# Windowed attention and a squared-ReLU MoE on one core: the first six P V products turned, the last first-product by Strassen, finer token units, another plan

## The chip, the cores and the metric

The kernel runs on one core of a Trainium2 chip. The metric is the device time in microseconds of one execution. Five engines take part: TensorE (PE, matrix products), VectorE (DVE), ScalarE (ACT), GpSimd (POOL, here it only issues loads that convert float32 to bf16) and SyncE (SP, here it only issues DMA transposes). Each engine works through its own list of instructions in order, and engines wait for one another by semaphores.

## What is computed

Two stages in a row: attention in a sliding window of 32 positions to either side, over 8 batches, 8 heads, 576 positions and 64 dimensions; then, on the 4608 tokens of 512 features that come out, two products with a squared ReLU between them.

```python
scores = scale * np.matmul(q, k.transpose(0, 1, 3, 2))
mask = np.abs(pos[:, None] - pos[None, :]) <= window
scores = np.where(mask, scores, -1000000000.0)
attn = np.exp(scores - np.max(scores, axis=-1, keepdims=True))
attn = attn / (np.sum(attn, axis=-1, keepdims=True) + 1e-09)
x = np.matmul(attn, v)             # -> [4608, 512]
h = x @ w_in                       # [512, 2048]
r = np.maximum(h, 0.0)
out = (r * r) @ w_out              # [2048, 512]
```

## The kernel before

**Attention** goes in 24 steps `G` of 192 queries (three to a batch). Keys and queries of a step are loaded by POOL (`load_qk`, L357), turned so that the head dimension lies on the partitions (`turn_pe` on the PE for the first two batches, `turn_dma` by DMA transposes on SP for the others), and multiplied in two windows of 128 keys, `w` = 0 and 1 (`scores`, L465). ScalarE takes the exponential. For steps 0 to 2 the mask is added in the PE as a bias; for the others DVE multiplies by it (L515). The probabilities lie in `pt`, keys on partitions, queries in columns, eight heads beside each other.

`pv` (L519) multiplies with `pt` as the weights and the values as the moving side, 65 columns a head: 64 of values and one of ones, which gives the sum of the row. So queries come out on partitions, and one reciprocal of 8 sums (L550) with a multiplication of 512 columns (L553) a window normalises them into `xa` and `xb`. The MoE needs them the other way, features on partitions, in the ring `xt` of 1536 tokens. `xturn` (L558) does that: for steps 0 to 5 by eight PE transposes (L570, L575) and one eviction by ScalarE (L580), for the others by two DMA transposes on SP (L584, L587).

**The MoE's first product** (`mm1`, L592) fills one PSUM bank of 512 columns at a time (`ht`, two of them): a unit is 192 tokens by 2 feature blocks up to token 768, 256 by 2 up to 1024, and 512 by 1 after that. ScalarE takes the ReLU into `rt` (four of them), DVE squares it into the ring `gt` of 1024 tokens (L614). **The second product** is plain for the first 512 tokens (`mm2`, L618, matmuls at L625). From there each 512 tokens are a 2 x 2 block product by Strassen's scheme with seven products (`strassen`, L694; matmuls at L687). DVE makes its sums of weights once (`sums_w2`, L648) and its sums of `gt` for every tile (`sums_g`, L663).

**The order of the work** is written out by a planner at build time. Every operation is recorded with an engine, what it reads and writes, an assumed duration and a key; `schedule` (L92) plays it through and gives each engine a fixed list. Keys of the attention steps are `3 * G + OG[G] - LEAD`, of their loads `3 * G + OL[G] - LEAD - AHEAD`, of the Strassen tiles `8 * g + LS + OS[g]`; the first product's key is its first token over 64. `move=(rounds, ns)` is a DMA's assumed length. Loads from the third batch on may also not be issued before the PE operation that had last been recorded (`after=self.moe`). In the gaps that the plan shows for the PE before 40 us it inserts matmuls on zeros (L294).

The constants that the change touches:

```python
NSPLIT = 6     # steps whose two windows are scored one after the other
NXT = 6        # steps whose result is turned on the PE
LEAD = 10.0
def dve(n, fast=True):
    return 153 + (0.52 if fast else 1.04) * n
```

Of the kernel before, what the change touches and what calls it, by code (L numbers as in the profile page):

```python
# [5 lines left out]
ALU = mybir.AluOpType  # L6
# [12 lines left out]
RING = 1536  # L19
GRING = 1024  # L20
NSTD = 4
BIAS = 74.0
LS = 10.75
OG = [-0.75, -0.25, -2.0, -2.75, -0.25, 2.25, 4.0, 1.25, 2.0, 1.75, 3.0, 0.75, 0.25, -0.25, -0.5, 0.25, -0.5, -2.0, -2.25, -3.0, 2.75, 1.25, -4.25, 3.0]
OL = [3.0, 1.0, 4.5, 5.5, 2.5, -0.5, -2.0, -3.5, -3.5, -0.5, 0.0, -0.5, -1.0, -3.5, -1.5, 1.5, -0.5, -3.5, -3.5, -1.0, 2.0, 1.0, -3.0, -6.5]
OS = [-4.0, 4.5, -2.0, 2.0, 1.75, 3.25, 4.5, 5.25, 4.5]
NV, NRAW = 6, 6
NTURN = 2
NXT = 6
LEAD = 10.0  # L30
# [19 lines left out]
class Prog:  # L50
# [11 lines left out]
    def rec(self, eng, fn, reads=(), writes=(), dma=None, dur=100, key=0.0, move=0, name="", after=None, slack=0):  # L62
        op = Op()
        op.eng, op.fn, op.dma, op.dur, op.key, op.move, op.name = eng, fn, dma, dur, key, move, name
        op.deps, op.order = set(), set()
        op.inc, op.val, op.sem = False, None, None
        op.slack = slack
        op.lat = self.LAT[eng]
        for r in reads:
            w = self.writer.get(r)  # L70
            if w is not None:
                (op.order if w.eng == eng == "PE" else op.deps).add(w)
        for t in writes:
            w = self.writer.get(t)
            if w is not None:
                (op.order if w.eng == eng and w.dma is None and dma is None else op.deps).add(w)
# [12 lines left out]
        self.ops.append(op)  # L89
        return op  # L90

    def schedule(self):  # L92
# [37 lines left out]
        def serve(until):  # L130
            nonlocal now, spent
            while now < until:
# [117 lines left out]
class Gen:  # L250
# [5 lines left out]
    def alloc(self):  # L256
# [11 lines left out]
        self.MASK = [sb(f"mask{i}", [128, 128], BF16) for i in range(4)]  # L268
        self.BIAS = [sb(f"bias{i}", [128, 128], BF16) for i in range(4)]
        self.ID = sb("ident", [128, 128], BF16)  # L270
        self.E = [sb(f"e{i}", [128, 1024], BF16) for i in range(2)]
        self.PT = [sb(f"pt{i}", [128, 8, 128], BF16) for i in range(3)]
        self.RS = [sb(f"rs{i}", [128, 8], F32) for i in range(4)]
        self.XA = [sb(f"xa{i}", [128, 512], BF16) for i in range(3)]
# [7 lines left out]
        self.UE = [sb(f"ue{i}", [128, 512], F32) for i in range(2)]  # L282
        self.RT = [sb(f"rt{i}", [128, 512], BF16) for i in range(4)]
# [29 lines left out]
    def setup_mask(self, i, key):  # L313
# [19 lines left out]
        else:  # L333
            p.writer[hi[0]] = last
            p.readers[hi[0]] = []

# [110 lines left out]
    def turn_dma(self, t, b, g, key):  # L447
# [14 lines left out]
    def mask_of(self, g, w):  # L462
        return w if not (g == 0 and w == 0 or g == 2 and w == 1) else w + 2

    def scores(self, G, ws):  # L465
# [8 lines left out]
        def f(e):  # L474
            for w in ws:
                k0 = a + 128 * w
                mi = self.mask_of(g, w)
# [5 lines left out]
                for j in range(4):  # L483
                    for par in range(2):
                        r = 64 * par
                        q = qt[r:r + 64, j, a + 64:a + 192]
                        if w == 0:
# [10 lines left out]
        rd += ["id"] + [("bias", self.mask_of(g, w)) for w in ws] if pm else []  # L498
# [3 lines left out]
        for w in ws:  # L502
            n = 2 * G + w
            sc = self.AT[:, 1024 * reg[w]:1024 * reg[w] + 1024]
            e_, pt = self.E[n % 2], self.PT[n % 3]
            if pm:
                self.p.rec("ACT", lambda e, pt=pt, sc=sc: e.activation(pt[:].rearrange("p h q -> p (h q)"), sc, ACTF.Exp, scale=0.125),
                           reads=tags[w], writes=[("pt", n % 3)], key=key, dur=act(1024), name=f"X{G}{'AB'[w]}")
# [3 lines left out]
            mi = self.mask_of(g, w)  # L512
# [3 lines left out]
                       reads=[("e", n % 2), ("mask", mi)], writes=[("pt", n % 3)], key=key, dur=dve(1024),  # L516
                       name=f"M{G}{'AB'[w]}")

    def pv(self, G, w):  # L519
# [3 lines left out]
        reg = 1 if G < NSPLIT else 0  # L523
        c0 = 1024 * reg
        vt, pt, avp = self.V[G % NV], self.PT[n % 3], self.AT
# [13 lines left out]
        rd = [("v", G % NV, w), ("vset", G % NV), ("pt", n % 3), "zz"]  # L539
# [17 lines left out]

    def xturn(self, G):  # L558
# [3 lines left out]
        wr = [("xt", (3 * G + c) % (RING // 64)) for c in range(3)]  # L562
        if G < NXT:
            ps, bank = self.AT[:, 1024:1536].bitcast(BF16), self.half(2)
            if G < 3:
                ps, bank = self.OUTP[0][:].bitcast(BF16), ["outp0"]

            def f0(e):
                for j in range(4):
                    mm = e.transpose(ps[:, 192 * j:192 * j + 64], xa[64:128, 128 * j:128 * j + 128], self.ID[64:128, 64:128])  # L570
                return mm

            def f1(e):
                for j in range(4):
                    mm = e.transpose(ps[:, 192 * j + 64:192 * j + 192], xb[:, 128 * j:128 * j + 128], self.ID[:])  # L575
                return mm

            self.p.rec("PE", f0, reads=[("xa", G % 3), "id"], writes=bank, key=key, dur=150, name=f"T{G}a")
            self.p.rec("PE", f1, reads=[("xb", G % 3), "id"] + bank, writes=bank, key=key, dur=230, name=f"T{G}b")
            self.p.rec("ACT", lambda e: e.activation(self.XT[:, :, r:r + 192],  # L580
                                                     ps[:, 0:768].rearrange("p (j q) -> p j q", j=4), ACTF.Copy),
                       reads=bank, writes=wr, key=key, dur=act(768), name=f"XT{G}")
            return
        self.p.rec("SP", lambda e: e.dma_start(self.XT[:, :, r:r + 64], xa[64:128, :], transpose=True),  # L584
                   reads=[("xa", G % 3)], writes=wr[:1], dma=(f"xa{G % 3}", G), key=key - 0.3, dur=TISS, move=(16, 20), name=f"T{G}a",
                   slack=TSLACK)
        self.p.rec("SP", lambda e: e.dma_start(self.XT[:, :, r + 64:r + 192], xb[:], transpose=True),  # L587
                   reads=[("xb", G % 3)], writes=wr[1:], dma=(f"xb{G % 3}", G), key=key, dur=TISS, move=(32, 20), name=f"T{G}b", slack=TSLACK)
# [3 lines left out]
    def mm1(self, t0, n, ds, key):  # L592
# [16 lines left out]
        self.moe = self.p.rec("PE", f, reads=[("xt", s) for s in steps] + [("w1", d0 // 4)], writes=[f"ht{k % 2}"], key=key,  # L609
# [8 lines left out]
    def mm2(self, u, seg, key):  # L618
# [14 lines left out]
        if seg == 3:  # L633
# [4 lines left out]
                       reads=[("oe", u % 4)], writes=[("out", u)], dma=(f"o{u % 4}", u), key=key, dur=600, move=(8, 80), name=f"st{u}")  # L638

    def sums_w2(self, key):  # L640
        w, t, p = self.W2, self.TS, self.p
        for c in range(2):
            k, k8 = slice(4 * c, 4 * c + 4), slice(8 + 4 * c, 12 + 4 * c)
            b11, b12, b21, b22 = w[:, k, 0:256], w[:, k, 256:512], w[:, k8, 0:256], w[:, k8, 256:512]
            for i, a, b, rd in ((0, b12, b11, [("w2", c)]), (2, b22, b12, [("w2", c), ("w2", 2 + c)]),
# [3 lines left out]
                      writes=[("t", i, c)], key=key, dur=dve(1024), name=f"w{i}{c}")  # L649

# [43 lines left out]
    def strassen(self, g, key):  # L694
# [5 lines left out]
        def out(i, j, rd, fn, eng, k, name):  # L700
# [7 lines left out]
                  writes=[("out", u)], dma=(f"o{u % 4}", u), key=k, dur=600, move=(16, 45), name=f"st{u}")  # L708
# [18 lines left out]
    def build(self):  # L727
        p = self.p
        self.k1 = 0
# [6 lines left out]
        self.setup_mask(2, K + 1)  # L736
# [5 lines left out]
        self.setup_mask(0, K + 4)  # L742
        self.setup_mask(3, K + 5)
        for n, i in enumerate((2, 1, 0, 3)):
# [22 lines left out]
        for G in range(NG):  # L767
# [12 lines left out]
            for w in range(2):  # L780
                at(base + 0.3 * w + 0.1, self.pv, G, w)
            at(base + 0.5, self.xturn, G)
        t0 = 0
        while t0 < NTOK:
            n = 192 if t0 < 768 else 256 if t0 < 1024 else 512
            m = 512 // n
            for x, d in enumerate(range(0, 16, m)):
# [54 lines left out]
```

## Time and profile before

| what | us |
|---|---|
| median of three runs | 316.83 |
| the three runs | 310.51, 316.90, 316.83 |
| the profiled execution | 312.76 |
| its span, first to last instruction | 310.8 |
| idle matmuls on zeros (L294), 183 of them | 13.7 busy |
| sixth step's eviction to `xt` (L580) ends | 68.81 |
| last matmul of the first product starts | 286.2 |

Durations of operations that the text uses, mean of one: 

| operation | ns |
|---|---|
| reciprocal, 128x8 from PSUM (L550) | 208 |
| normalising multiplication, 128x512 from PSUM (L553) | 689 |
| mask multiplication, 128x1024 bf16 (L515) | 691 |
| square, 128x384 / 128x512 bf16 (L614) | 355 / 422 |
| sums of 128x1024 bf16 (L648, L663) | 679 to 686 |
| key copy from PSUM, 640 / 768 bf16 columns (L444) | 492 / 558 |
| eviction of `xt`, 128x768 (L580) | 808 |
| ScalarE, 128x512 from PSUM (L611, L698) | 599, 602 |

"Busy" of the PE counts each matmul until its result is written, so neighbouring ones overlap; the pace of a chain of matmuls is read from the start of one to the start of the next. The granted clock is that of the PE, as a share of full speed. In the waits "issue" is time for which the profile shows no releaser.

### The profile page before, as it was taken

How to read it: one execution, taken by the hardware profiler on the slowest of the kernel's cores; microseconds unless marked ns; L12 is line 12 of the kernel's file. 1: busy time of each engine (PE TensorE's matmuls, PEld its weight loads, DVE VectorE, ACT ScalarE, POOL GpSimd, SP SyncE). 2: the span in 40 equal slices, each digit the busy share in tenths (PEclk: the TensorE clock that was granted, in tenths of full speed). 3: DMA queues.
4: the chain of work that ended last, by engine and by line, in shares of the span. 5: the costliest groups of instructions: out<-in, count | busy, mean ns of one | idle time of the engine just before them, and what ended most of it. 6: DMA issues, size and time to landing. Idle time of an engine off the chain costs nothing.

```text
span 310.8 us, 7401 instructions
## 1 busy us (share of the span) xinstructions
PE 292.8 (94%) x2993; PEld 205.6 (66%) x3027; DVE 192.6 (62%) x420; ACT 166.7 (54%) x260; POOL 117.6 (38%) x153
## 2 busy tenths in 40 slices
PE   6899999999799999999999499999979999999995
PEld 6788776868685567556667455586548556666874
DVE  7135766645986896598539636695549765743701
ACT  3546657747536765746675156625762575355230
POOL 8999457308355650299114002992000000000000
PEclk9999999999999999999999979999999999999999
DMA  9999999999999999999999922999974311201123
GB/s 150 167 206 197 187 153 155 190 170 135 143 169 199 157 161 163 94 151 146 173 144 145 210 41 60 123 156 193 169 97 62 88 41 24 71 34 36 64 71 103
DMA packets 179553, 40.37 MB, mean 130 GB/s; under 512 B 166720, under 2 KB 179008, under 8 KB 179520
## 3 DMA queue, kind: packets, MB, share of 16 engines
q0 software_dynamic: 121920, 18.98, 92.7%
q1 hardware_dynamic: 46752, 11.09, 28.1%
q10 hardware_dynamic: 10848, 9.83, 11.4%
q8 instruction: 24, 0.39, 0.5%
q14 instruction: 9, 0.07, 0.1%
HBM read 38.80 MB, written 9.44 MB: 155 GB/s over the span
## 4 chain that ended last, share of the span: by engine, by line
PE 68%; issue 10%; DMA 8%; POOL 6%; DVE 4%; ACT 1%; SPq 1%; POOLq 0%; ACTq 0%; DVEq 0%
PE ht L605 30%; PE outp L687 23%; DMA kraw<-in_k_dram 5%; PE outp L625 4%; PE at L535 4%; PE at L489 3%; POOL kraw L365 2%; POOL qraw L365 2%; POOL v L396 2%; DMA v<-in_v_dram 2%; DMA qt<-qraw 2%; PE outp L294 2%; DVE ss L663 1%; DVE gt L614 1%; ACT rt L611 1%
## 5 line engine op out<-in xcount | busy, mean ns | idle before, releaser
L605 PE MATMUL ht<-xt,w 128*128 128x512 bf16 (+2 forms) x741 | 136.8, 326 | 6.1 <-issue 4.6
L611 ACT ACTIVATE rt<-ht 128x512 bf16<-128x512 f32 (+1 forms) x152 | 86.5, 576 | 74.4 <-PE ht L605 65.4
L605 PEld LDWEIGHTS ht<-xt,w 128*128 128x128 bf16 x768 | 68.6, 98 | 48.7 <-issue 5.6
L614 DVE TENSOR_TENSOR gt<-rt 128x512 bf16<-128x512 bf16 (+1 forms) x152 | 61.5, 408 | 59.0 <-ACT rt L611 56.6
L365 POOL DMA_DIRECT2D kraw<-in_k_dram x46 | 36.2, 809 | 92.6 <-issue 47.6
L510 ACT ACTIVATE e<-at 128x1024 bf16<-128x1024 f32 x42 | 41.4, 1021 | 11.0 <-PE at L489 11.0
L396 POOL DMA_DIRECT2D v<-in_v_dram x48 | 41.5, 891 | 0.1
L515 DVE TENSOR_TENSOR pt<-e,mask 128x1024 bf16<-128x1024 bf16 x42 | 29.0, 691 | 18.3 <-ACT e L510 18.2
L365 POOL DMA_DIRECT2D qraw<-in_q_dram x46 | 36.3, 810 | 0.5 <-issue 0.5
L687 PE MATMUL outp<-w,gt 128*128 128x256 bf16 x256 | 32.2, 273 | 0.7 <-ACT outp L698 0.7
L687 PE MATMUL outp<-ts,ss 128*128 128x256 bf16 x256 | 31.7, 273 | 0.3 <-DVE ss L663 0.3
L687 PE MATMUL outp<-ts,gt 128*128 128x256 bf16 x256 | 31.6, 273 | 0.0
L687 PEld LDWEIGHTS outp<-w,gt 128*128 128x128 bf16 x256 | 24.7, 98 | 7.7 <-ACT outp L698 1.1
L687 PEld LDWEIGHTS outp<-ts,ss 128*128 128x128 bf16 x256 | 24.4, 98 | 5.9 <-DVE ss L663 0.4
L687 PEld LDWEIGHTS outp<-ts,gt 128*128 128x128 bf16 x256 | 24.6, 98 | 4.2
L535 PEld LDWEIGHTS at<-v,pt 128*64 128x64 bf16 (+1 forms) x576 | 17.1, 106 | 12.6 <-issue 4.2
L535 PE MATMUL at<-v,pt 128*64 128x65 bf16 (+1 forms) x576 | 20.8, 196 | 2.8 <-DVE xa L553 1.7
L550 DVE RECIPROCAL rs<-at 64x8 f32<-64x8 f32 (+1 forms) x48 | 10.0, 209 | 15.3 <-PE at L535 14.0
L489 PEld LDWEIGHTS at<-qt,kt 64*128 64x128 bf16 x384 | 10.8, 94 | 11.1 <-issue 10.5
L489 PE MATMUL at<-qt,kt 64*128 64x128 bf16 x384 | 15.9, 218 | 1.8 <-DMA qt<-qraw 1.8
L553 DVE TENSOR_TENSOR xa<-at,rs 64x512 bf16<-64x512 f32 x24 | 16.7, 695 | 0.8
L553 DVE TENSOR_TENSOR xb<-at,rs 128x512 bf16<-128x512 f32 x24 | 16.5, 689 | 0.7
(65 smaller groups left out, 218.6 us busy)
## 6 DMA issues: line engine op xcount, KB each, us to landing
out_dram<-oe ACTq DMA_DIRECT2D x36, 256.0 KB, 4.5
qraw<-in_q_dram POOLq DMA_DIRECT2D x46, 96.0 KB, 8.6
v<-in_v_dram POOLq DMA_DIRECT2D x32, 128.0 KB, 10.6
w<-in_moe_w_in_dram POOLq DMA_DIRECT2D x4, 512.0 KB, 9.4
w<-in_moe_w_out_dram POOLq DMA_DIRECT2D x4, 512.0 KB, 16.6
kraw<-in_k_dram POOLq DMA_DIRECT2D x14, 112.0 KB, 12.9
kraw<-in_k_dram POOLq DMA_DIRECT2D x16, 96.0 KB, 6.0
v<-in_v_dram POOLq DMA_DIRECT2D x16, 96.0 KB, 12.0
```

Of the source, the lines that this page charges most:

```text
L365: self.p.rec("POOL", lambda e, j=j: e.dma_start(raw[0:h, j, :].rearrange("p (h d) -> p h d", h=8), s[:, j]), writes=[("raw", t, G % NRAW, ...
L396: self.p.rec("POOL", lambda e, j=j, lo=lo, hi=hi, k0=k0: e.dma_start(vt[lo - k0:hi - k0, j, :, 0:64], self.v[b, :, lo:hi, :].rearrange("h ...
L489: mm = e.matmul(sc[:, 512 * par + 128 * j:512 * par + 128 * j + 128], kt[r:r + 64, j, k0:k0 + 128], q, start=not pm, stop=True, skip_group ...
L510: self.p.rec("ACT", lambda e, e_=e_, sc=sc: e.activation(e_[:], sc, ACTF.Exp, scale=0.125), reads=tags[w], writes=[("e", n % 2)], key=key, ...
L515: self.p.rec("DVE", lambda e, pt=pt, ee=ee, mb=mb: e.tensor_tensor(pt[:], ee, mb, ALU.mult), reads=[("e", n % 2), ("mask", mi)], writes=[( ...
L535: mm = e.matmul(avp[z:z + n, c:c + 65], pt[:, 4 * (h % 2) + h // 2, z:z + n], vt[:, w, h, 0:65], start=((w == 0 or z == 64) and y == 0), s ...
L553: self.p.rec("DVE", lambda e: e.tensor_tensor(x[r0:128, :].rearrange("p (x y c) -> p x y c", x=2, y=4), av[:, :, :, 0:64], rb, ALU.mult), ...
L605: mm = e.matmul(ht[:, n * x:n * x + n], self.W1[:, ft, 128 * d:128 * d + 128], self.XT[:, ft, r:r + n], start=(ft == 0), stop=(ft == 3))
L611: self.p.rec("ACT", lambda e: e.activation(rt[:, 0:c], ht[:, 0:c], ACTF.Relu), reads=[f"ht{k % 2}"], writes=[("rt", k % 4)], key=key, dur= ...
L614: self.p.rec("DVE", lambda e: e.tensor_tensor(gt[:, d0:d0 + len(ds), rg:rg + n], rr, rr, ALU.mult), reads=[("rt", k % 4)], writes=[("gt", ...
L625: mm = e.matmul(op[:], gt[:, d, r:r + 128], self.W2[:, d, :], start=(d == 0), stop=(d == 15))
L687: mm = e.matmul(op[:, 256 * y:256 * y + 256], lhs[:, l0[0] + k, a:a + 128], rhs[:, r0 + k, c0:c0 + 256], start=start and y == 0 and k == 0 ...
```

## The change

Steps 0 to 5 get `pv_turned` in place of `pv` and `xturn`: the values are the weights, the probabilities move, and the result comes out with features on partitions. A second matmul with a block of ones as the weights gives the sums, repeated on all 64 partitions of the head, so the reciprocal is of 128x384 instead of 128x8. The multiplication writes `xt` directly. The two halves `x` (four heads each) use the same two PSUM banks.

```diff
+    def pv_turned(self, G, x):
+        key = 3 * G + OG[G] - LEAD + 0.3 + 0.1 * x
+        vt, pts, at = self.V[G % NV], [self.PT[(2 * G + w) % 4] for w in range(2)], self.AT
+        bank = self.half(2) + self.half(3)
...
+            for w in range(2):
+                for y in range(2):
+                    for par in range(2):
+                        h = 4 * x + 2 * y + par
+                        c = 192 * y + 64 * w
+                        for z, lhs in enumerate((vt[:, w, h, 0:64], self.ONES[:])):
+                            mm = e.matmul(at[64 * par:64 * par + 64, 1024 + 512 * z + c:1024 + 512 * z + c + 128], lhs,
+                                          pts[w][:, 4 * par + 2 * x + y, :], start=(w == 0 and y == 0), stop=True,
+                                          skip_group_check=True)
...
+        rq = self.RQ[x]
+        self.p.rec("DVE", lambda e: e.reciprocal(rq, at[:, 1536:1920]), reads=bank, writes=[("s", 0, x)],
+                   key=key, dur=dve(384, False), name=f"R{G}{'ab'[x]}")
...
+        self.p.rec("DVE", lambda e: e.tensor_tensor(dst, src, rq.rearrange("p (y q) -> p y q", y=2), ALU.mult),
```

For these steps window 0 takes its queries in their natural order, with two plain masks (4 and 5) beside the four old ones, and `pt` has four buffers instead of three.

The last 512 tokens' first product (`MSTART = 8`) becomes four units of Strassen's seven products, each on two PSUM banks of its own turn (`ht`, then two pairs of `at`). Sums of `w_in` are made once, into the buffers of the loaded keys and queries; sums of `xt` once; the two copies of a unit go to the `e` tiles.

```diff
+            if t0 >= 512 * MSTART:
+                if t0 == 512 * MSTART:
+                    at(t0 / 64 - 1, self.sums_w1, t0 / 64 - 1)
+                at(t0 / 64 - 0.5, self.sums_x, t0, t0 / 64 - 0.5)
+                for x in range(4):
+                    at(t0 / 64 + 2 * x, self.mm1_strassen, t0, 2 * x, x % 3, t0 / 64 + 2 * x + OM[x % 3])
...
+        product(1, ks[0])
+        copy(y, x, xtag, ytag, ks[0], f"sd{t0}.{d}")
+        product(2, ks[1])
+        direct(0, 0, x, xtag, ks[1])
+        product(6, ks[2])
+        copy(u2, y, ytag, [("e", 0)], ks[2], f"u{t0}.{d}")
+        product(5, ks[3])
+        copy(p5, x, xtag, [("e", 1)], ks[3], f"p{t0}.{d}")
+        product(7, ks[4])
+        added(1, 1, y, ytag, p5, [("e", 1)], ks[4])
+        product(3, ks[5])
+        added(0, 1, x, xtag, u2, [("e", 0)], ks[5])
+        product(4, ks[6])
+        direct(1, 0, y, ytag, ks[6])
```

`direct` is the ReLU on ScalarE and the square on DVE as before; `added` is an addition from PSUM and a squared ReLU, both on DVE.

Units of 256 tokens reach to token 2048 (`NFINE`) instead of 1024. The plan's constants are other ones, among them the lead and the assumed lengths of DMAs (`move`), and operations on ScalarE and DVE that overwrite what the same engine wrote or read now wait for it by semaphore.

```diff
-LEAD = 10.0
+LEAD = 11.5
-OG = [-0.75, -0.25, -2.0, -2.75, -0.25, 2.25, 4.0, 1.25, ...
+OG = [-3.75, -10.5, -4.75, -0.25, -3.0, -5.5, -7.5, -2.5, ...
-OL = [3.0, 1.0, 4.5, 5.5, 2.5, -0.5, -2.0, -3.5, ...
+OL = [7.5, 2.0, 5.0, -1.5, -1.0, -1.5, -0.5, 2.0, ...
-LS = 10.75
+LS = 8.25
...
-                if spent >= (120 if now < 30000 else 180 if q == "POOL" else 60):
+                if spent >= (400 if q == "POOL" else 200):
...
-                (op.order if r.eng == eng and r.dma is None else op.deps).add(r)
+                (op.order if r.eng == eng and eng not in ("ACT", "DVE") and r.dma is None else op.deps).add(r)
...
-                       dma=(f"t{t}{G % 6}", G), key=key, dur=TISS, move=(h // 4, 20), name=f"td{t}{b}{g}", slack=TSLACK)
+                       dma=(f"t{t}{G % 6}", G), key=key, dur=TISS, move=(h // 4, 22.6), name=f"td{t}{b}{g}", slack=TSLACK)
```

More of the change, by code (lines that the diff above doesn't have):

```diff
@@ L75, in rec @@
             if w is not None:
[L76 removed]
+                (op.order if w.eng == eng and eng not in ("ACT", "DVE") and w.dma is None and dma is None else op.deps).add(w)
             for r in self.readers.get(t, ()):
[L78 removed]
+                (op.order if r.eng == eng and eng not in ("ACT", "DVE") and r.dma is None else op.deps).add(r)
         if after is not None:
@@ L607, in f @@
             return mm
-        self.moe = self.p.rec("PE", f, reads=[("xt", s) for s in steps] + [("w1", d0 // 4)], writes=[f"ht{k % 2}"], key=key,
+        self.moe = self.p.rec("PE", f, reads=[("xt", s, x) for s in steps for x in range(2)] + [("w1", d0 // 4)], writes=[f"ht{k % 2}"], key=key,
                    dur=4 * len(ds) * (n / 2.4 + 2.5), name=f"A{t0}.{d0}")
@@ L735, in build @@
         self.setup_id(K)
-        self.setup_mask(2, K + 1)
+        self.ms("DVE", ["ones"], self.ONES[:], 1.0, K + 2)
+        self.setup_mask_plain(5, K + 1)
         self.setup_mask(1, K + 2)
```

204 lines of the change are left out of this document (154 added, 50 removed).

## The prediction

> **What bounds the kernel now.** I read the page first: engine shares, then the 40 slices.
>
> ```profile
> PE 292.8 (94%) x2993; PEld 205.6 (66%) x3027; DVE 192.6 (62%) x420; ACT 166.7 (54%) x260; POOL 117.6 (38%) x153
> ...
> PE   6899999999799999999999499999979999999995
> ...
> DVE  7135766645986896598539636695549765743701
> ACT  3546657747536765746675156625762575355230
> ```
>
> TensorE (PE) is the bound as a share, but not in every stage. The first four slices hold idle matmuls on `zz`; slices 23 and 29 (about 179-186 and 225-233 us) hold stalls. So I asked three stages separately: the opening, whose six attention steps the change rewrites; the stalls, which a new plan could move; and the last tile. For the opening, the busy time of each engine in stretches, and the timeline of PE around the sixth step:
>
> ```profile
> core 0: us, PE busy (x) PEld busy (x) DVE busy (x) ACT busy (x) POOL busy (x), PEclk, DMA share, GB/s
> 13.50:24.00 10.50, 10.45 (x177) 8.98 (x178) 4.35 (x10) 5.00 (x8) 10.50 (x14) 1.00 1.29 205
> 24.00:45.00 21.00, 20.89 (x274) 17.53 (x277) 14.18 (x33) 12.74 (x24) 13.78 (x18) 1.00 1.83 180
> 45.00:69.00 24.00, 23.41 (x301) 16.25 (x304) 14.31 (x32) 16.61 (x26) 9.46 (x12) 1.00 2.01 165
> ```
>
> ```profile
> 67.56 0.40 PE L575 MATMUL at<-ident,xb 128*128 128x128 bf16 x4
> 67.80 1.89 PE L625 MATMUL outp<-w,gt 128*128 128x512 bf16 x8
> 69.52 1.91 PE L605 MATMUL ht<-xt,w 128*128 128x256 bf16 x16
> ```
>
> From 13.5 to 69 us VectorE (DVE) is busy 4.35+14.18+14.31 = 32.8 of 55.5 us. The sixth step's `xt` is evicted from 68.00 to 68.81, and the first matmuls that read it start at 69.52, directly after the last L625 of the four plain output blocks: the PE has no other MoE work left. What delays the sixth step's `xt` delays the PE.
>
> The stall, from the timeline:
>
> ```profile
> 178.65 1.22 SPq L587 DMA_TRANSPOSE xt<-xb  x1
> ...
> 179.07 3.08 PE L605 MATMUL ht<-xt,w 128*128 128x512 bf16 x7 [4.28 <-issue]
> ```
>
> A tile's matmuls wait 4.28 us. No releaser is named; an `xt` transpose issued by SP at 170.93 is the last transfer that they need, so I read this as that transfer landing late. The seven matmuls then take 427 ns each by their weight loads (180.35 to 180.77), not 216: the granted clock is 0.89 over 176 to 192 us. Loss: 4.28 + 7 x 0.211 = 5.8 us. A second wait, 1.75 us before the scores at 229.38, names the query transpose.
>
> **The change, part by part.** All against the profiled execution: 312.76 us (span 310.8), which is 1.3% under the median of the three runs (316.83) and above their lowest (310.51).
>
> Turned P V, removed. Per step: two reciprocals and two multiplications on DVE (2 x (0.21 + 0.69) = 1.80 us), eight transposes on the PE and one 0.81 us eviction on ScalarE. Six steps: 10.8 us of DVE.
>
> Turned P V, added. Per half step: 16 matmuls of 128 columns, a reciprocal of 128x384 from PSUM, and a multiplication of 128x384. The multiplication: L553's 128x512 takes 690 ns; the key copies of 768 and 640 elements take 558 and 492, which leaves a fixed part of some 160 ns; so 1.035 ns per element, 160 + 384 x 1.035 = 0.56 us. The reciprocal has only this row:
>
> ```profile
> L550 DVE RECIPROCAL rs<-at 128x8 f32<-128x8 f32 x24 | 5.0, 208 | 4.2 <-PE at L535 3.3
> ```
>
> Eight elements should take 160 + 8 = 168 ns at one element a cycle; they take 208 to 211. The 41 to 49 ns above that are either a longer start, then 384 elements take 0.56 to 0.60 us, or a slope: (209 - 160)/8 = 6.1 ns an element, then 160 + 384 x 6.1 = 2.5 us. I take the slope, 2.5 us, because the fixed part of two other PSUM forms agrees and leaves no room for another; both ends stay for the range. The Trainium skill (VectorE: DVE Perf Modes, "First, the fixed hardware budget") says that Reciprocal runs as an iterative divide with a repeat count of 8; read as eight cycles an element it speaks against this change harder than my row does, and is a rival below.
>
> DVE then carries 12 x (2.5 + 0.56) = 36.7 us instead of 10.8: 32.8 + 25.9 = 58.7 us in a stretch of 55.5. DVE becomes the opening's bound. The order on each engine is fixed by a plan that books 0.55 us for this reciprocal, so nothing is rearranged for it.
>
> When is the sixth `xt` ready? Lower bound, DVE never idle: 13.5 + 58.7 = 72.2, 3.4 us late. Upper bound, nothing absorbed: 12 x 2.16 us (3.06 for 0.90) less six times the removed transposes and eviction (some 1.4 us from L575's start to L580's end): 25.9 - 8.4 = 17.5 late. Between: the first step's second exponential ends at 13.75; two halves of 1.0 (16 matmuls at 56 ns and handover) + 2.5 + 0.56 + 0.1, one after the other as both use one PSUM pair, end at 22.2 where the old eviction ended at 17.9. Steps four to six have scores at 45.2, 51.3 and 59.3, 7 us apart, and each asks DVE for 6.1 + 1.4 (two masks) + 0.56 (keys) + 2.84 (eight squares of 0.355) = 10.9 us. Three such from 45.2, behind some 2 us left over, end at 80: 11 us late. I take 11.
>
> What comes back: PE idles 2.0 us from 69 to 94, and runs no L605 from 80.3 to 93.5, because a 512-token unit needs step eight; the 256-token units need only the next step. I give back 3 us. Net of the opening: +8, bounds 0.4 to 17.5. The extra matmul time (32 x 56 ns against some 0.85 us a step, +0.9) lies in PE waits for DVE; without that cover it is 5 us.
>
> Other edits of the opening. The plain masks and `ones` are a few DVE instructions of 0.1 to 0.3 us before 6 us; the first scores wait for the key copy ending at 9.63, so 0. The self-waits on DVE and ScalarE are for operations long done; a dependent DVE pair shows a gap of 0.03 us, and both engines have idle time: 0. If that cover is gone on DVE in the opening, its 75 instructions there make 2.3 us.
>
> The new plan, 256-token units to token 2048. Unit sizes change no PE time: 16 matmuls of 256 take 1.75 us, 8 of 512 take 1.73. LEAD rises by 1.5 steps, and transposes are planned 13% longer, so `xt` and scores' transfers are issued earlier against the PE. That aims at 5.8 + 1.75 = 7.5 us of stalls. I take 60%, -4.5; bounds: all, -7.5, and a new stall of the middle size, +3, as every load and every queue is reordered (POOL's loads, SP's transposes, ScalarE's stores). What is late next are the scores' own transposes, behind each other on SP at 1.2 us each.
>
> Last tile by Strassen. 64 matmuls of 512 at 216 ns (13.8 us) become 112 of 256 at 109 (12.2) and two of 0.22: -1.2 us. DVE gains 8 x 0.69 + 4 x 0.42 for sums, and per unit 2 x 1.38 + 2 x 0.42 instead of 4 x 0.42: +15 us from about 262 to 286, where it was busy under half. The chain of a unit through the two shared `e` tiles is two copies of 0.60, two products of 0.44 with 0.2 handovers and an add of 0.69: some 3.1 us; four fit in the 21 us in which other products fill the PE. I take -1.2; if that filling runs out, +2.
>
> Sum: 312.8 + 8 - 4.5 - 1.2 = 315.1 us. That is 0.7% over the profiled execution and 0.5% under the median.
>
> **The rivals.**
> (a) The reciprocal runs one element a cycle: 0.56 us. DVE gets +2.6 us, the first `xt` comes at 18.3, the opening loses nothing and the finer units give 2: 312.8 - 2 - 4.5 - 1.2 = 305. For it: nothing in the trace measures the slope. Against: the 41 ns. Chance 0.15.
> (b) The PE's fixed order, slower. The second half's matmuls stand in PE order where the plan expects the first half's multiplication; everything behind them waits too. If each reciprocal's lateness blocks the head of PE's queue, the opening loses the full 17.5 and gives back little (2): 312.8 + 17.5 - 2 - 1.2 = 327 with stalls that stay, 323 with half of them gone. It decides once the plan has under 2 us of other PE work between the halves. For: L625 stands directly before L605 with nothing spare. Against: from 45 to 69 us some 8.0 us of L605 and 10.4 us of L625 stood between the steps, and can cover such a wait. Chance 0.24.
> (c) The stalls stay or move: 315.1 + 4.5 = 319.6. Chance 0.15.
> (d) Eight cycles an element: 8 x 1.035 x 384 + 160 = 3.34 us, 0.84 more each, 10 us on a DVE that is full: 325. Against: eight elements would then take 226 ns and take 209. Chance 0.06. [...]
> My forecast holds 0.40; its own range is 308 to 322.
>
> **How the numbers follow.** Two per cent (6.3 us) is about what a measurement of this kernel tells from no change: its three runs spread that far. Taken from 312.8: faster is under 306.5, slower over 319. Faster: (a)'s 0.14 and 0.09 from the forecast's and (c)'s low ends, 0.23. Slower: (b) 0.23, (d) 0.06, half of (c) 0.06 and the forecast's upper end 0.05, 0.40. Same: 0.37. The forecast is 315; the range, 304 to 326, reaches (a), (c), (d) and half of (b).
>
> **What would show it.** The 128x384 reciprocal's mean: 2.5 us supports the sum; 0.6 makes it (a). DVE nearly full from 14 to 80 us; PE waiting there for DVE at the turned matmuls or at L605's successor; the sixth `xt` near 80. Reciprocals of 2.5 us with the sixth `xt` before 73 would make the opening wrong; idle PE over 15 us before 90 makes it (b). No PE wait over 2 us between 165 and 235 shows the plan right. The last tile's `w1` sums over by 270 and no PE gap over 0.5 us before 290 show the Strassen part.

## The result, and the profile after

| | before | changed |
|---|---|---|
| median of the runs, same chip | 313.67 us (310.22 to 316.9, 4 runs) | 322.36 us (320.89 to 323.91, 4 runs) |
| ratio to before, 95% interval | 1 | 1.0387 [1.0304, 1.047] |
| profiled execution, its span | 312.76, 310.8 us | 322.49, 320.5 us |

The changed kernel is slower by 3.9%; two of the old kernel's four runs (316.90 and 316.83 us) fell in a slow state, so this ratio is taken to the other two (310.51 and 310.22 us). Between the two profiled executions the difference is 9.7 us, where the forecast had 2.3. The page's first two parts, of the changed kernel:

```profile
PE 296.2 (92%) x3194; PEld 222.6 (69%) x3194; DVE 231.1 (72%) x446; ACT 164.8 (51%) x258; POOL 117.4 (37%) x153
...
PE   7977979867797999999998999999999999999995
...
DVE  8268697799588675967963899659869834788921
```

DVE is busy 38.5 us longer, the PE 3.4. Counted from 0, the PE's row is all 9s only from slice 13 on (104 us; one 8 and the last slice excepted). From slice 2 to 12 it mixes 6s, 7s and 8s with 9s, where the old kernel's row had 9s and one 7. Slices 22 and 29, which held the old kernel's stalls, are now 9s (the prediction's "23" is slice 22 when counted this way). The disputed instruction has its own group (fifth part of the page; count, busy time, mean ns, idle time before and its cause):

```profile
L602 DVE RECIPROCAL ss<-at 128x384 f32<-128x384 f32 x12 | 30.7, 2557 | 8.7 <-PE at L592 8.6
```

2557 ns each; the multiplication behind it (L607) takes 556 (median). Busy time by stretch, as in the prediction, and one stretch more:

```profile
13.50:24.00 10.50, 8.19 (x135) 5.58 (x132) 5.82 (x4) 4.97 (x6) 10.50 (x14) 1.00 1.25 202
24.00:45.00 21.00, 18.14 (x223) 14.25 (x224) 17.13 (x28) 9.23 (x18) 16.33 (x22) 1.00 1.84 179
45.00:69.00 24.00, 20.32 (x248) 14.27 (x247) 19.55 (x28) 12.30 (x20) 2.20 (x3) 1.00 1.62 144
69.00:94.00 25.00, 19.43 (x237) 14.43 (x234) 19.79 (x29) 11.29 (x19) 12.24 (x16) 1.00 1.02 76
```

The PE (first pair) is busy 8.1 us less than before from 13.5 to 69 (46.65 against 54.75). DVE (third pair) is busy 42.5 of 55.5 us there, 77%: not full. Both idle, because they wait for each other. The timelines of PE and of DVE at the sixth step show how, one half after the other:

```profile
77.38 0.83 PE L637 MATMUL ht<-xt,w 128*128 128x192 bf16 x8
78.05 1.03 PE L657 MATMUL outp<-w,gt 128*128 128x512 bf16 x4
80.70 0.25 PE L592 MATMUL at<-pt,v 128*64 128x128 bf16 x2 [1.62 <-DVE xt L607]
...
81.27 1.90 PE L657 MATMUL outp<-w,gt 128*128 128x512 bf16 x8
84.68 1.91 PE L637 MATMUL ht<-xt,w 128*128 128x256 bf16 x16 [1.51 <-DVE xt L607]
```

```profile
77.50 2.56 DVE L602 RECIPROCAL ss<-at 128x384 f32<-128x384 f32 x1 [0.20 <-PE at L592]
80.09 0.56 DVE L607 TENSOR_TENSOR xt<-at,ss 128x384 bf16<-128x384 f32 x1
80.56 0.35 DVE L646 TENSOR_TENSOR gt<-rt 128x384 bf16<-128x384 bf16 x1
81.39 2.56 DVE L602 RECIPROCAL ss<-at 128x384 f32<-128x384 f32 x1 [0.48 <-PE at L592]
83.98 0.56 DVE L607 TENSOR_TENSOR xt<-at,ss 128x384 bf16<-128x384 f32 x1
```

The second half's matmuls start at 80.70, when the first half's multiplication has released the one PSUM pair; between the two halves the PE's list holds only the 1.7 us from 77.38 to 79.08. Then come 0.6 us of matmuls, the reciprocal, the multiplication: a half every 3.9 us, here and at 17 to 33 us alike. In PE's fixed order only one block of 1.90 us lies between the second half and the next reader of `xt`, so the PE waits again until 84.68. Before, the same reader started at 69.52. The waits from 12 to 100 us (engine, what, releaser: total us, times, longest):

```profile
POOL kraw L383 <- PE ht L637: 38.8, 3, 25.8
...
PE at L592 <- DVE xt L607: 9.3, 7, 1.6
...
PE ht L637 <- DVE xt L607: 4.1, 3, 1.6
```

Ten waits of the PE for a multiplication, 13.4 us. In the first line the total says little: in the same stretch POOL waited 30.4 us for the PE before the change, and 32.2 in e1_copy, below. What matters is when a wait ends. POOL's loads wait for PE work that is late here, so they start late: the key load that e1_copy issues at 61.75 us is issued at 72.99. From 69 to 94 the core moves 76 GB/s where it moved 157.

To see where time is lost and won, I counted the MoE work done on the PE by a given moment (its weight loads, each at its matmul's pace: 0.0825, 0.109 and 0.216 us for 192, 256 and 512 columns) and took the difference to the old kernel. The changed kernel's total is 1.4 us less, the Strassen part. Its arrears:

| us from the start | 40 | 69 | 94 | 130 | 165 | 200 | 240 | 270 | 290 |
|---|---|---|---|---|---|---|---|---|---|
| arrears in us | 3.0 | 6.7 | 10.7 | 12.5 | 15.2 | 10.2 | 9.0 | 9.8 | 11.0 |

So 10.7 us are lost by 94 and another 4.5 by 165; 5.0 come back from 165 to 200, where the old kernel had its long stall, and 1.2 by 240, where it had the second. The 11.0 at 290 less the 1.4 are, to 0.1, the 9.7 of the spans. Not all of the 4.5 is owed to the opening: by the same count e7_plan_only and e2_oldpv, whose openings are in time, lose 4.5 and 3.5 from 94 to 165 too, and e1_copy, which has the changed kernel's lists, 0.8. And 1.7 us of it are a lower clock: from 100.7 to 104.1 us the granted clock is 0.50, shortly after a wait of 1.77 us of the PE for DVE (up to 99.41). The old kernel has 3.4 us at 0.50 as well, from 178.5 to 181.9, in its long stall.

### The profile page after: what moved, and what is told of

It is laid out like the page before. It is cut to its first block, busy times and chain, and to the rows that moved or that the text cites. A ratio compares the mean times of both kernels' runs of the same rounds, so it can differ in the third digit from the quotient of the medians.

```text
span 320.5 us, 7818 instructions
## 1 busy us (share of the span) xinstructions
PE 296.2 (92%) x3194; PEld 222.6 (69%) x3194; DVE 231.1 (72%) x446; ACT 164.8 (51%) x258; POOL 117.4 (37%) x153
## 4 chain that ended last, share of the span: by engine, by line
PE 79%; DVE 14%; DMA 4%; issue 1%; ACT 1%; POOL 0%; POOLq 0%; ACTq 0%
PE ht L637 34%; PE outp L827 28%; DVE ss L602 9%; PE at L512 4%; PE at L557 3%; DMA xt<-xa 3%; PE at L592 2%; PE ht L735 2%; PE at L735 2%; DVE xt L607 2%; DMA qraw<-in_q_dram 2%; PE outp L301 2%; PE outp L657 1%; PE at L450 1%; DVE ts L680 1%
## 5 line engine op out<-in xcount | busy, mean ns | idle before, releaser
L637 PE MATMUL ht<-xt,w 128*128 128x256 bf16 (+2 forms) x832 | 124.3, 298 | 5.5 <-DVE xt L607 4.1
L643 ACT ACTIVATE rt<-ht 128x512 bf16<-128x512 f32 (+1 forms) x136 | 76.8, 575 | 69.6 <-PE ht L637 59.0
L637 PEld LDWEIGHTS ht<-xt,w 128*128 128x128 bf16 x832 | 74.0, 98 | 36.5 <-DVE xt L607 3.6
L383 POOL DMA_DIRECT2D kraw<-in_k_dram x46 | 35.8, 790 | 138.8 <-PE ht L637 58.7
L646 DVE TENSOR_TENSOR gt<-rt 128x512 bf16<-128x512 bf16 (+1 forms) x136 | 54.2, 405 | 34.3 <-ACT rt L643 32.9
L538 DVE TENSOR_TENSOR pt<-e,mask 128x1024 bf16<-128x1024 bf16 x42 | 28.7, 689 | 13.3 <-ACT e L533 13.2
L602 DVE RECIPROCAL ss<-at 128x384 f32<-128x384 f32 x12 | 30.7, 2557 | 8.7 <-PE at L592 8.6
L827 PE MATMUL outp<-ts,ss 128*128 128x256 bf16 x256 | 33.2, 279 | 0.3 <-DVE ss L803 0.3
L827 PE MATMUL outp<-w,gt 128*128 128x256 bf16 x256 | 32.2, 273 | 0.8 <-ACT outp L838 0.7
L557 PEld LDWEIGHTS at<-v,pt 128*64 128x64 bf16 (+1 forms) x432 | 13.0, 106 | 7.6 <-issue 5.9
L838 ACT ACTIVATE ue<-outp 128x512 f32<-128x512 f32 x16 | 9.6, 599 | 16.1 <-PE outp L827 16.1
L557 PE MATMUL at<-v,pt 128*64 128x65 bf16 (+1 forms) x432 | 15.5, 196 | 1.8 <-DVE xa L575 1.8
L592 PE MATMUL at<-pt,v 128*64 128x128 bf16 x96 | 7.0, 225 | 10.3 <-DVE xt L607 9.3
## 6 DMA issues: line engine op xcount, KB each, us to landing
w<-in_moe_w_out_dram POOLq DMA_DIRECT2D x4, 512.0 KB, 16.8
```

Source lines behind the costliest of these rows:

```text
L383: self.p.rec("POOL", lambda e, j=j: e.dma_start(raw[0:h, j, :].rearrange("p (h d) -> p h d", h=8), s[:, j]), writes=[("raw", t, G % NRAW, ...
L538: self.p.rec("DVE", lambda e, pt=pt, ee=ee, mb=mb: e.tensor_tensor(pt[:], ee, mb, ALU.mult), reads=[("e", n % 2), ("mask", mi)], writes=[( ...
L557: mm = e.matmul(avp[z:z + n, c:c + 65], pt[:, 4 * (h % 2) + h // 2, z:z + n], vt[:, w, h, 0:65], start=((w == 0 or z == 64) and y == 0), s ...
L592: mm = e.matmul(at[64 * par:64 * par + 64, 1024 + 512 * z + c:1024 + 512 * z + c + 128], lhs, pts[w][:, 4 * par + 2 * x + y, :], start=(w ...
L602: self.p.rec("DVE", lambda e: e.reciprocal(rq, at[:, 1536:1920]), reads=bank, writes=[("s", 0, x)], key=key, dur=dve(384, False), name=f"R ...
L637: mm = e.matmul(ht[:, n * x:n * x + n], self.W1[:, ft, 128 * d:128 * d + 128], self.XT[:, ft, r:r + n], start=(ft == 0), stop=(ft == 3))
```

## The experiments

Ratios are to the kernel before, run on the same chip beside it, with 95% intervals; the changed kernel's is 1.0387. Differences in us between two experiments are between their medians. Three questions: is it the reciprocal, by which way does it act, and what are the other parts worth.

**e1_copy: no division.**

```diff
-        self.p.rec("DVE", lambda e: e.reciprocal(rq, at[:, 1536:1920]), ...
+        self.p.rec("DVE", lambda e: e.tensor_copy(rq, at[:, 1536:1920]), ...
```

> The changed kernel with the wide reciprocal (128x384, twelve times, 2.56 us each) replaced by a copy of the same size, same plan; the division of the first six steps is left out (they are multiplied by their sums). Theory A, the reciprocal's own length lies on the opening's serial chain and is the whole loss: the copy takes 0.56 us, 12 x 2.0 = 24 us leave DVE, the sixth xt is ready by 69 us or before instead of 84.5, and the kernel comes to 305 to 308 us, under the kernel before. Rival B, the turned form or the new plan loses the opening by itself (two halves in one PSUM pair, PE order): it stays above 314 and the sixth xt stays later than 76.

Measured: 305.15 us (303.98 to 305.73), ratio 0.985 [0.9805, 0.9895]. The same group in its page:

```profile
L602 DVE COPY ss<-at 128x384 f32<-128x384 f32 x12 | 6.7, 557 | 10.8 <-PE at L592 10.5
```

The copy takes 557 ns, which is what the plan books for the reciprocal (552). Every engine's list is that of the changed kernel, instruction by instruction. The multiplications and one of the later key loads, in the changed kernel (first of each pair) and in e1_copy:

```profile
L607 DVE TENSOR_TENSOR xt<-at,ss x12: 544/556/558, 20.4 to 84.0; 128x384 bf16<-128x384 f32 x12
L607 DVE TENSOR_TENSOR xt<-at,ss x12: 549/557/558, 18.2 to 68.0; 128x384 bf16<-128x384 f32 x12
107.29 1.53 POOL L383 DMA_DIRECT2D kraw<-in_k_dram  x2 [11.49 <-PE at L557]
90.10 1.54 POOL L383 DMA_DIRECT2D kraw<-in_k_dram  x2 [9.93 <-PE at L557]
```

The last multiplication starts at 68.0 instead of 84.0, and the time falls by 17.2 us. This key load starts 17.2 us earlier, and all that follow it 17.2 to 18.5. All of the loss, and more, hangs on 12 x 2.0 us. This kernel leaves out the division, so it is no candidate; it marks what turning these steps in this order could reach if a division cost no more than a copy.

**e2_oldpv: the turned P V and its masks undone, everything else kept.**

```diff
-                for x in range(2):
-                    at(base + 0.4 + 0.1 * x, self.pv_turned, G, x)
+                for w in range(2):
+                    at(base + 0.3 * w + 0.1, self.pv, G, w)
+                at(base + 0.5, self.xturn, G)
```

> The changed kernel with the first six steps' P V, their masks and their turning on the PE as before; Strassen, finer units and the new constants stay, the plan is made anew by the same planner. Theory A: the loss is in the turned P V alone, so 305 to 309 us, sixth xt near 69. Rival B, the new constants or the finer units lose the opening: above 314.

Measured: 309.88 us (307.5 to 311.41), ratio 0.9975 [0.9934, 1.0017], a little over the first expectation and far from the second. The loss is in the turned P V; the other edits together make no difference that can be measured.

**e3_known: the plan told the length.** The same operations in another order, with more matmuls on zeros.

```diff
-                   key=key, dur=dve(384, False), name=f"R{G}{'ab'[x]}")
+                   key=key, dur=2557, name=f"R{G}{'ab'[x]}")
```

> The changed kernel, but the planner books 2557 ns for the wide reciprocal instead of 552, so each engine's list is made for its true length. Theory A, the length itself is the cost: only part of the PE's 13.4 us of waits for the multiplication into xt is filled, 316 to 321 us. Rival C, the loss comes from lists fixed under a wrong duration (second half's matmuls at the head of the PE's queue): 312 us or less.

Measured: 315.32 us (314.37 to 316.74), ratio 1.0187 [1.0137, 1.0237]: between the two expectations. Busy time by stretch, e3_known:

```profile
13.50:69.00 55.50, 55.13 (x729) 41.77 (x734) 45.09 (x60) 29.93 (x48) 30.77 (x40) 1.00 1.66 169
69.00:94.00 25.00, 18.54 (x236) 14.51 (x235) 21.41 (x39) 11.43 (x19) 12.32 (x16) 0.97 1.46 120
```

The rearranged order keeps the PE busy up to 69 us (55.13 of 55.5), with DVE busier than in the changed kernel. Not all of that is useful: of the PE's 8.5 us more, 3.9 are matmuls on zeros (L301, 8.94 against 5.02), which the planner puts into the gaps that it now sees. By the count of MoE work the arrears are 2.0 us at 69, where they were 6.7. But the last multiplication still starts at 78.7, the PE idles 6.5 us from 69 to 94, and at 94 the arrears are 7.4. So of the 17.2 us between e1_copy and the changed kernel, 7.0 go with an order made for a wrong length, and 10.2 remain with this order, which knows it.

**e8_beside: the reciprocals beside the chain.** e1_copy, with two reciprocals of 128x384 on scratch data behind each step's second half; no result of theirs is used.

```diff
+    def beside(self, G):
+        for x in range(2):
+            self.p.rec("DVE", lambda e: e.reciprocal(self.DUM[:, 384:768], self.DUM[:, 0:384]), reads=[("xt", 3 * G % (RING // 64), 1), "dumset"],
+                       writes=["dum"], key=3 * G + OG[G] - LEAD + 0.5, dur=1, name=f"D{G}{x}")
...
+                at(base + 0.55, self.beside, G)
```

> As e1_copy (the division of the first six steps is left out), but after each step's second half DVE also does two reciprocals of 128x384 on a scratch tile that nobody reads; every other instruction stands in the order of e1_copy. DVE then carries the changed kernel's load and 12 copies more, but the reciprocals lie beside the chain from one half to the next. Theory A1, the serial chain is the cost: 305 to 311 us. Theory A2, DVE is simply full in the opening, as the prediction put it: 317 us or more. e1_copy measured 305.15, the changed kernel 322.36.

Measured: 324.52 us (323.68 to 327.1), ratio 1.0474 [1.0358, 1.059]. DVE's timeline and the waits:

```profile
62.17 0.68 DVE L539 TENSOR_TENSOR pt<-e,mask 128x1024 bf16<-128x1024 bf16 x1
62.77 5.13 DVE L614 RECIPROCAL dum<-dum 128x384 f32<-128x384 f32 x2
67.82 0.63 DVE L539 TENSOR_TENSOR pt<-e,mask 128x1024 bf16<-128x1024 bf16 x1
```

```profile
PE at L593 <- DVE pt L539: 7.9, 2, 4.0
```

The time is in the range of theory A2, but not for its reason: DVE is busy 44.8 of 55.5 us from 13.5 to 69, so it is not full here either. Taken off the chain of P V, the same 12 x 2.56 us stand in DVE's queue ahead of the next step's mask multiplication, and the PE waits for that. So the loss is not a matter of the one PSUM pair alone: DVE works in order, and in this place too what stands behind the reciprocals is late. The granted clock was 0.80 from 69 to 94 us in this run, so its time holds more than these waits.

**e11_ownbanks: the second half in banks of its own**, for the first two steps.

```diff
         bank = self.half(2) + self.half(3)
+        if x == 1 and G < 2:
+            bank, o, z_ = ["ht0", "ht1"], self.HT[0][:], self.HT[1][:]
```

> The changed kernel, correct, with one thing altered: in the first two steps the second half's P V and sums go to the two PSUM banks of `ht` instead of the pair that the first half still holds, so the second half's matmuls need not wait for the first half's multiplication. In the changed kernel the four halves of these steps follow each other every 3.90 us (reciprocals at 17.79, 21.68, 25.57, 29.47), of which 0.74 us are VectorE waiting for the PE. Theory A (the chain through one PSUM pair is a part of the loss): two of the three 0.74 us waits between the four halves go, the fourth multiplication starts about 1.5 us earlier (30.6 against 32.06), the TensorE's order is laid out anew by the planner, and the time falls by 1 to 3 us, 319 to 321. Theory B (VectorE's time itself is the bound, or what is won here is waited for at the third step): the fourth multiplication comes earlier but the sixth step's last one stays at 84 (within 0.7 us) and the time is 321 to 324. Above 324 the two `ht` banks, which the first MoE units and the query transposes also use, cost more than the pair did.

Measured: 329.96 us (329.05 to 330.41), ratio 1.0563 [1.044, 1.0686]. Within a step the chain does break: the reciprocals stand at 16.92 and 19.40, back to back, with no wait between. But the PE's timeline shows what the banks cost:

```profile
22.82 0.82 PE L450 MATMUL ht<-ident,qraw 96*128 96x96 bf16 x8 [3.44 <-DVE xt L610]
38.09 0.51 PE L450 MATMUL ht<-ident,qraw 96*128 96x96 bf16 x8 [3.51 <-DVE xt L610]
```

The query transposes use `ht`, and at the head of PE's queue they wait 3.5 us for the multiplication; the second step's reciprocals begin at 32.20 instead of 25.57. Neither expectation held; the case above 324 did. The two waits are not all of that. The granted clock was 0.50 from 22.1 to 28.9 and from 39.1 to 42.5 us, near the ends of these waits, and this plan put 13.2 us of matmuls on zeros between 13.5 and 45 (5.0 in the changed kernel), which the PE runs in their place even when it is late. So this run does not tell what the one PSUM pair costs; it shows that in a fixed order a bank freed in one place can become a wait in another.

**e4_lnexp: the division on ScalarE**, as exp(-ln s); the trace has one table load, so both functions came from one set.

```diff
-        self.p.rec("DVE", lambda e: e.reciprocal(rq, at[:, 1536:1920]), ...
+        self.p.rec("ACT", lambda e: e.activation(rq, at[:, 1536:1920], ACTF.Ln), ...
+        self.p.rec("ACT", lambda e: e.activation(rq, rq, ACTF.Exp, scale=-1.0), ...
```

> The changed kernel with the wide reciprocal as exp(-ln(s)) in two ScalarE instructions of 128x384, one activation table that holds both functions; the plan is made for it. If the reciprocal's 2.56 us is the loss, two instructions of some 0.5 us (175 + 0.833 x 384 ns by the planner, 0.49 us) in its place cost 12 x 0.5 = 6 us against e1_copy where nothing covers them: 306 to 311 us, and DVE loses 30.7 us of work. Rival: ScalarE, which also evicts the MoE's banks, is late for them: above 313 us.

Measured: 310.97 us (309.79 to 314.35), ratio 1.0026 [0.9975, 1.0076]. By line, from the trace (count: least, median and greatest ns, first and last start):

```profile
L606 ACT ACTIVATE ss<-at x12: 484/491/491, 18.0 to 71.0; 128x384 f32<-128x384 f32 x12
L608 ACT ACTIVATE ss<-ss x12: 514/523/526, 18.5 to 72.1; 128x384 f32<-128x384 f32 x12
```

1.01 us in place of 2.56, on an engine that had room. 11.4 of the 17.2 us are back. The sixth `xt` is 4.7 us later than in e1_copy (last multiplication from 72.7), which is most of the 5.8 us that remain. It is level with the kernel before.

**e7_plan_only: the kernel before, with only the new constants** (`BIAS`, `LS`, `OG`, `OL`, `OS`, `LEAD`, the lengths in `move`, the queue turns).

> The kernel before with nothing changed but the plan's constants (lead, offsets, DMA lengths, ring turns). Theory A, the new plan removes the late stalls whatever the opening does: the waits near 175 and 227 us (5.8 and 1.75 us) go, 306 to 309 us. Rival D, the constants fit only the kernel they were searched for: 313 us or more, with other stalls.

Measured: 312.86 us (312.78 to 313.11), ratio 1.0105 [1.0073, 1.0137]: no gain, close to the second expectation. By the count of MoE work it is 2.0 us in arrears at 69, 0.4 at 94, 4.9 at 165, 0.7 at 200: the stall near 180 is gone, and what that brings was lost before.

**e9_before_fine: the kernel before, with 256-token units to token 2048 and the self-waits.**

```diff
-            n = 192 if t0 < 768 else 256 if t0 < 1024 else 512
+            n = 192 if t0 < 768 else 256 if t0 < 2048 else 512
```

> The kernel before with two things of the change alone: 256-token units up to token 2048 in place of 1024, and the self-waits on ScalarE and VectorE; its old constants, old P V and plain last tile are kept. Theory A: the gain of the finer units that the changed kernel shows (5.7 us between e6_coarse and the changed kernel) comes from giving the TensorE something to read while the opening's xt is late, so it shrinks where the opening is not late: 0 to 3 us faster than before, ratio 0.99 to 1.00. Theory B: the finer units are worth their 5.7 us in any opening: ratio 0.98 to 0.985. If the self-waits cost something (I booked them at nothing), it is slower than before; over 1.005 would show that.

Measured: 311.81 us (310.16 to 315.11), ratio 1.0104 [1.0016, 1.0192]. No gain. By the expectation a ratio over 1.005 would be a cost of the self-waits, but I leave it open: the interval almost reaches 1, e2_oldpv has the self-waits too and is at 0.9975, and self-waits and units were not run apart.

**e6_coarse: the changed kernel with the fine units only to token 1024** (`NFINE = 1024`).

> The changed kernel with units of 512 tokens from token 1024 again (the plan is made anew). By the prediction's step the finer units give 2 to 3 us near the ninth step: 324 to 326 us. Rival: they give nothing here: 321 to 323 us.

Measured: 328.07 us (327.24 to 329.08), ratio 1.0565 [1.0476, 1.0655]: 5.7 us over the changed kernel, more than either theory had. But not in the opening: at 94 us both have the same MoE work left (191.9 us in e6_coarse, 192.2 in the changed kernel), at 200 it is 111.2 against 106.9. It lies at 165 to 200:

```profile
165.00:200.00 35.00, 32.40 (x305) 18.80 (x304) 23.13 (x48) 17.43 (x28) 14.24 (x18) 0.95 1.70 159
```

There the PE of e6_coarse is busy 32.40 us at a granted clock of 0.95, that of the changed kernel 33.73 at 1.00. The trace shows a wait of 1.75 us for a mask multiplication before 176.65, and soon after it a granted clock of 0.50 from 177.0 to 180.4 us, where eight matmuls of 512 columns take 3.55 us in place of 1.90. These two are some 3.4 us; the changed kernel has one wait of 1.27 us there. Why DVE was late I did not trace.

**e10_oldpv_finer: e2_oldpv with fine units to token 3072** (`NFINE = 3072`).

> As e2_oldpv (the turned P V undone, everything else of the change kept), with 256-token units up to token 3072 in place of 2048. Theory A: past the opening nothing is late, so more fine units change nothing: 308 to 311, ratio 0.99 to 1.00 to the kernel before. Theory B: finer units keep paying: under 307.

Measured: 310.12 us in the one run with a granted clock of 0.999, and 316.54 to 319.34 us in three with 0.977 to 0.984. One run is too little for a ratio, and this stays open.

**e5_nostrassen and e12_oldpv_nostr: the last tile plain again** (`MSTART = 9`), in the changed kernel and in e2_oldpv.

> The changed kernel with the last tile's first product plain again. By the prediction's step Strassen is worth 1.2 us: 323.0 to 324.2 us, and 13.8 us of PE pace in that tile instead of 12.2 + 0.4. Rival: its chains of copies and adds cost what they save: 322 us or less.

> As e2_oldpv, with the last 512 tokens' first product plain as before in place of Strassen's. Theory A: the Strassen part takes 1.6 us of TensorE work away and the end of the kernel is bound by the TensorE once the opening is not late, so this is 1 to 2 us slower than e2_oldpv, 311 to 312. Theory B: what it saves is lost again in its waits for VectorE, as e5_nostrassen (0.8 us faster than the changed kernel, within its spread) suggests: 309 to 310.5.

Measured: 321.55 us (321.48 to 322.09), ratio 1.0358 [1.0275, 1.044], and 309.39 us (308.08 to 311.36), ratio 0.9974 [0.9937, 1.0011]. Against their partners (1.0387 and 0.9975) neither shows a gain by Strassen, and both lie in the ranges of the second expectations; an interval of 0.4% is 1.2 us, all that was forecast. The spans of the profiled executions say more: e12_oldpv_nostr has 307.4 and e2_oldpv 306.1, 1.3 less with Strassen, and up to 270 us their arrears differ by 0.7 us at most. In the changed kernel the count gives Strassen's 1.6 us too, but by 240 us its plan has lost 2.8 against e5_nostrassen's.

## Why the prediction was right or wrong

The forecast of 315 was wrong; the result lies in the range, in the slower case, where rival (b) had put it. The error, 7.3 us, lies in the opening's term: its lateness was forecast some 5 us too small, and the 3 us that were to come back did not.

- **The reciprocal's length: right.** 2.5 us forecast by the slope, 2557 ns measured; the multiplication 0.56, measured 0.555. Rival (a), with 0.56 us, falls; e1_copy shows its time, 305.15, where it said 305. So close a hit is partly luck: (a) also counts on the -4.5 of the plan and the -1.2 of Strassen, and e2_oldpv finds next to nothing of their sum (0.9975). The 4.7 us between e1_copy and e2_oldpv, which the turned P V saves when no division is paid, make up for that. Rival (d) falls too: from 128x8 to 128x384 it is (2557 - 208)/376 = 6.25 ns an element, six cycles of 1.035 ns and not eight. The Trainium skill (VectorE: DVE Perf Modes, "First, the fixed hardware budget") gives a repeat count of 8; read as eight cycles an element, the estimate would have been 3.34 us, and the measurement decides against that reading.
- **"DVE becomes the opening's bound": right in what is waited for, wrong in how.** I added DVE's busy time to the stretch, 58.7 of 55.5. It was busy 42.5. The bound is the alternation: matmuls, reciprocal, multiplication, and the next half only then. e8_beside shows that reciprocals in DVE's in-order queue delay the PE as well when that alternation is short.
- **The sixth `xt`: mis-sized.** 80 forecast between 72.2 and 86.3; 84.5 measured, 15.7 us later than before. What the middle estimate left out is a half's 3.9 us cycle in a chain with the PE's order, instead of a queue of DVE work that is never idle.
- **"What comes back: I give back 3 us": the step that failed.** Nothing came back. The cleanest control is e1_copy, with the same lists and a short operation in the reciprocal's place: its last multiplication starts 16.0 us earlier and its time is 17.2 us less. The forecast and rival (a), which differ by the reciprocal's length and what follows from it, had 10 us between them (315.1 and 305); the 7.2 us that are missing are about the forecast's whole error, some 5 of them lateness and the rest what did not come back. Against the old kernel the opening was booked net at +8: the sixth `xt` is 15.7 us later, the arrears are 10.7 us at 94 and 15.2 at 165 (in part perhaps the plan's, as said above). I took the 256-token units for other work that fills the wait. But the order is fixed before the run, with 1.90 us of other work where 3.4 us are waited, and the loads of the next steps wait for the late PE work: in e1_copy the key loads start 11.2 us earlier (61.75 for 72.99), then 17.2 (90.10 for 107.29), and from there on never less. e6_coarse shows no gain of the units before 94 us.
- **Rival (b), the PE's fixed order: seen.** Its condition, under 2 us of other work between the halves, is met at the sixth step by the 1.7 us from 77.38 to 79.08; its sign, over 15 us of idle PE before 90, by 16.8 us (6.0 before); its places are the ten PE waits; its prices were 327 and 323, measured 322.4. Its loss of 17.5 us for the opening is near the 17.2 of e1_copy. It is not the whole: with an order that knows the length (e3_known) 10.2 of 17.2 us remain. I gave it 0.24 because L605 and L625 work "can cover such a wait"; e3_known shows that it covers most of it up to 69 us (arrears of 2.0 for 6.7) if the plan puts it there, and that the PE idles again after.
- **The late stalls, -4.5: right in direction, mis-sized.** The arrears show 5.0 + 1.2 = 6.2 us back, and of waits from 165 to 235 one of 1.27 is left:

```profile
170.19 1.90 PE L637 MATMUL ht<-xt,w 128*128 128x512 bf16 x8 [1.27 <-DMA xt<-xa]
```

 Rival (c), as far as its stalls stay, falls. But e7_plan_only shows that on the old kernel the same constants lose as much earlier (4.5 us from 94 to 165), so the term was no net gain of the plan; how much of the changed kernel's own 4.5 us there has moved in this way stays open. Of the 6.2 us, 1.7 are the old kernel's half clock. LEAD's 1.5, which I read as steps, are units of 64 tokens, so half a step.
- **Strassen, -1.2:** supported by a span (1.3) and by the count of work, not resolved by the times. The PE has no wait over 0.5 us from 262 to 290, and the sums of `w_in` are over at 230, both as forecast.
- **Masks, `ones` and self-waits, 0:** e2_oldpv holds all but `ones` and the plain masks and is level with before; e9_before_fine leaves room for a cost of the self-waits up to 1.9%.

## What to carry to other kernels

Before an element-wise operation moves from 8 columns to 384, measure it at 384: a slope from one short row, with the fixed part of other rows taken off, was worth more than the plan's formula, and it could be seen before the run. When a plan is fixed in advance, an operation nearly five times longer than booked can cost twice, once by its length and once by the order (here 10 and 7 us); tell the planner first, then judge the edit. A delay early on is not "filled" by finer units unless something in the queues is free to start, so look at who waits for the late work, loads above all. A busy PE is no proof of useful work where a plan fills gaps with matmuls on zeros; count the work itself.

## What the runs showed of the hardware

A DVE reciprocal of f32 costs 6.25 ns for each element of a partition's row (from 128x8 and 128x384), 2557 ns for 128x384 from PSUM; from SBUF, two took 5.13 us in e8_beside, the same. The copy of that shape took 557 ns. Logarithm and exponential on ScalarE took 491 and 523 ns: for this tile 1.01 us against 2.56. In several traces the granted clock falls to 0.50 for 3.4 us near the end of a wait of the PE, between 0.6 us before it and 1.3 us after: a wait of 4.28 us in the old kernel (to 179.07, the clock from 178.5), of 1.77 in the changed one (to 99.41, from 100.7), of 1.75 in e6_coarse (to 176.65, from 177.0). Other waits, like that of 1.62 us before 80.70 in the changed kernel, have none behind them, and no run here shows what decides. No version here beats the kernel before by more than its interval: e2_oldpv and e12_oldpv_nostr are at 0.9975 and 0.9974, with 1 inside both; only e1_copy, without the division, is clearly faster.
